# An adaLN block with linear attention and a GEGLU FFN on one core: the first token pair of the down projection, and where VectorE's extra work stands in the FFN units

## The chip, the cores and the metric

The kernel runs on one core of a Trainium2 chip. The metric is the device time of one execution in microseconds (us), the median of several runs. The profile shows one more execution, taken by the hardware profiler.

## The reference

```python
x = A_x                                    # [1, 2048, 1024], bf16
sa, ca, ga, sb, cb, gb = split(silu(c) @ w_mod, 6)
h = layernorm(x) * (1 + ca) + sa
x = x + ga * linear_attention(h, wqkv, wo)           # 32 heads
h = layernorm(x) * (1 + cb) + sb
x = x + gb * ((gelu(h @ w_gate) * (h @ w_up)) @ w_down)   # 1024 -> 3584 -> 1024
return x
```

The change concerns the last two lines: the second LayerNorm's scaling, the up and gate products (the FFN units) and the down projection.

## The kernel before

Every instruction is recorded with `sch.op` or `sch.dma` on one of five in-order streams (PE is TensorE, A is ScalarE, V is VectorE, G is GpSimd, Q is SyncE, called SP in the profile). The recorder derives each wait from the bytes that an instruction reads and writes. In the stages told here each stream runs in the order in which the Python code records it. DMAs leave from SP in order, on eight lanes in turn; a DMA also waits for the one before it on its lane.

**The FFN units.** The 2048 tokens are two halves p of 1024, and each half has 14 units; a unit v (0 to 27) computes 256 of the 3584 hidden columns for 1024 tokens with a 2x2 block scheme that needs seven products instead of eight. `unit` records them in the order P1, P5, P6, P2, P7, P3, P4, each of eight matmuls (`prod`, L1464): four for gate (t = 0), four for up (t = 1). P1 and P2 are bf16 on the tokens' h2 tiles and the raw weights; the other five are fp32r on sums: `s_sum` (L1418) makes sums of h2 tiles once for each half (eight VectorE instructions for p = 1), `t_sum` (L1438) makes sums of weights for every unit. The products add up in PSUM banks BA, BE, BB, BC (0, 2, 4, 6, plus t). Between them stand, for each t:

- after P1: `pcp` (ScalarE, L1470) copies BA to BB, on which P6 then adds; for t = 1 it must wait until the held product of the unit before (below) has read that bank
- after P5: `escp` (ScalarE, L1473) copies BE to ES
- after P6: `padd` (VectorE, L1476) writes BC = BB + ES; P7 then adds on BB, so it waits for padd
- after P7: `padd` writes BE = BB + ES; P4 then adds on BB
- after P2, P7, P3, P4: `gelu` (ScalarE, L1481) and the product gelu times up, `y_out` (VectorE, L1485). The product after P4 is held: it is recorded after P1 of the next unit.

`y_store` writes y to a DRAM scratch, `scr_y`. Extra work is hung into a unit with `hook(v, k, f)`: f is recorded when product k of unit v and its own steps have been recorded. VectorE's order around a unit's border is thus: product after P7, hook 7, product after P3, t_sum, hook 4, held product, t_sum twice, hook 5, padd. The extra work is:

- `mod2` (VectorE, L754): scales h2 of the second half by cb and sb, one instruction of 512 columns for each of eight 128-row blocks dc, for h = 0 (first 512 tokens) and h = 1. The h2 tiles arrive by transposing DMAs after `ln2_rows` (hook 3 of units 1 to 8). `mod2_act` is the same on ScalarE.
- `s_sum` for the second half, and `ar_copy` (ScalarE), a copy of an h2 block
- `b_sum` (L1577; its third step on ScalarE, L1571): sums of the down projection's weights, for K pairs 0 to 7. `raw_load(k)` loads the raw weights of K pair k (bx: the first 512 output columns, wst: the last 512).

**The down projection.** y has 3584 columns: 14 K pairs k of 2 x 128. Eight token pairs j of 256 tokens (two rows s of 128) are computed in order, with 1024 output columns in two halves c. For K pairs 0 to 12 (NST = 13) the seven products are used (`dprod`: P1, P5, P6, P2, P7, P3, P4, one matmul for each K pair); the rest is plain (`plain`: two matmuls for each K pair, row and half). `dpcp` (L1644), `descp` (L1648) and `dpadd` (L1652) are pcp, escp and padd here, and `a_sum` (VectorE, L1605; number 4 on ScalarE, L1599) makes the sums of y: numbers 0 and 2 in buffer XS 0 (for P5, then P7), 1 and 3 in XS 1 (P6, then P3), 4 in XS 2 (P4). Even pairs use banks 0, 2, 4, 6, odd pairs 1, 3, 5, 7. `devac` is two VectorE steps (L1675, L1676) and the store of 128 x 512 outputs. `x1_load` brings the residual in one of seven slots.

y lies in two buffers YL (l = 0, 1), one for all pairs: `y_load(j, l, k0, k1)` (L1586) loads a range of K pairs as soon as the pair before has used that range.

In pair 0 only K pairs 0 to 5 (NEA = 6) use the seven products: their weight sums are made in the units. K pairs 6 to 13 are plain, 64 matmuls, and meanwhile VectorE makes the weight sums of K pairs 8 to 12 (`lws(n)`: the next n steps), partly over pages that held raw weights which plain matmuls must have read first. Before the change the plain matmuls stand in four blocks of 16, one for each row and half, between the products: P1, P5, P6, P2, plain(0,0), P7, P3, plain(0,1), plain(1,1), P4, plain(1,0). The last block reads y of K pairs 6 to 13 for row 1, so the loads of y for pair 1 come late there:

```python
                if j == 1:
                    y_load(1, 0, NEA, NKP, P, 256)
                    y_load(1, 1, NEA, NKP, P, 256)
                    x1_load(j, 3)
                    a_sum(0, NEA, NST)
```

Of the kernel before, what the change touches and what calls it, by code (L numbers as in the profile page):

```python
# [10 lines left out]
P = 128  # L11
# [4 lines left out]
CPG = NCH // NSG  # L16
SGW = P * CPG
NDC = D // P
# [46 lines left out]
NKP = NFP  # L65
NST = 13
# [280 lines left out]
def bass_adaLN_cond__linear_attn_block__geglu_ffn__prompt_kernel(  # L347
# [18 lines left out]
    with ExitStack() as es:  # L366
# [133 lines left out]
        def r_h2(p, h, k0=0, k1=NDC, s0=0, s1=SGW):  # L500
            return r_t8(OFF_H2[p][h], f"h2{p}{'ab'[h]}", k0, k1, s0, s1)
# [243 lines left out]
        def h2ap(ph, dc, s0, s1):  # L745
            return H2[ph[0]][ph[1]][:, dc, s0:s1]
# [30 lines left out]
        def mod2(p, h, c0, n, dc0=0, dc1=NDC):  # L777
            mods(h2ap, r_h2p, (p, h), sc2, c0 * P, (c0 + n) * P, dc0, dc1, "h2")

        def mod2_act(h, c0=0, n=CPG, dc0=0, dc1=NDC):  # L780
            s0, s1 = c0 * P, (c0 + n) * P
            for dc in range(dc0, dc1):
                sA, sB, rs_ = sc2(dc)
                ap = h2ap((0, h), dc, s0, s1)
                sch.op(A, lambda e, ap=ap, sA=sA, sB=sB: e.activation(ap, ap, ACTF.Identity, bias=sB, scale=sA),
                       rd=r_h2(0, h, dc, dc + 1, s0, s1) + rs_, wr=r_h2(0, h, dc, dc + 1, s0, s1), note=f"h2modb {h}.{dc}")


        MC0 = 496
# [496 lines left out]
        def pq_scale(sg, h, gs):  # L1286
            i, t0 = sg % 2, h * HW
            for g0, g1 in gs:
                ap = PQ[sg][:, g0:g1, t0:t0 + HW]
                rng = r_pq(sg, g0, g1, t0, t0 + HW)  # L1290
                sch.op(V, lambda e, ap=ap, i=i, h=h, g0=g0, g1=g1: e.tensor_tensor(ap, ap, RB[i][:, h, g0:g1, :], ALU.mult),
                       rd=rng + r_rb(i, h, g0, g1), wr=rng, deps=rb_ops[sg, h], note=f"pqs{sg}.{h}.{g0}")
# [109 lines left out]
        def ar_copy(p):  # L1402
            for k in (0, 2):
                sch.op(A, lambda e, k=k: e.activation(A22R[p][:, k:k + 2, :], H2[p][1][:, ND2 + k:ND2 + k + 2, :], ACTF.Copy),
                       rd=r_h2(p, 1, ND2 + k, ND2 + k + 2), wr=r_ar(p, k, k + 2), note=f"arcp {p}.{k}")
# [17 lines left out]
        def t_sum(u, k):  # L1423
            if k == 3:
                ap, rd = wq(u, 1, 1)
                for t in range(2):
                    sch.op(A, lambda e, t=t: e.activation(TP[3][:, t, :, :], ap[:, t, :, :], ACTF.Copy), rd=rd[t:t + 1], wr=r_tp(3, t, t + 1), note=f"brcp u{u}")
                return
            if k == 0:
                (in0, r0), (in1, r1) = wq(u, 0, 1), wq(u, 0, 0)  # L1430
            elif k == 1:
                (in0, r0), (in1, r1) = wq(u, 1, 1), (T32[0], r_tp(0))
            elif k == 2:
                (in0, r0), (in1, r1) = wq(u, 1, 1), wq(u, 0, 1)
            else:
                (in0, r0), (in1, r1) = wq(u, 1, 0), (T32[1], r_tp(1))
            for t in range(2):
                sch.op(V, lambda e, t=t: e.tensor_tensor(TP[k][:, t, :, :], in0[:, t, :, :], in1[:, t, :, :], ALU.subtract),  # L1438
                       rd=r0[t:t + 1] + (r1[t:t + 1] if len(r1) == 2 else [(r1[0][0] + t * 2048, r1[0][0] + (t + 1) * 2048, r1[0][2])]),
                       wr=r_tp(k, t, t + 1), note=f"tsum{k} u{u}")  # L1440
# [58 lines left out]
        def hook(v, k, fn):  # L1499
            HK.setdefault((v, k), []).append(fn)  # L1500
# [179 lines left out]
        def cb1():  # L1680
# [6 lines left out]
                6: lambda: (mod2(0, 0, 0, 2), x_dma(10, 12)),  # L1687
                7: lambda: (t_sum(0, 0), t_sum(0, 1), pq_scale(2, 1, GH[0] + GH[1]), x_dma(12, 14)),
                8: lambda: mod2(0, 0, 2, 2),
                9: lambda: (pq_scale(3, 0, GH[0] + GH[1]), t_sum(0, 3), mod2_act(1, 0, 2), mod2_act(1, 2, 2, ND2)),  # L1690
                10: lambda: (t_sum(0, 4), t_sum(0, 2), rb_load(3, (1,)), x_dma(14, 16), row_load(GBB, R_GBB, 2, 0, "gbb", o_gb[0]), wt_dma(1)),
                11: lambda: None,
                12: lambda: (s_sum(0, 0, 0), mod2(0, 1, 2, 2, 0, ND2)),
# [18 lines left out]
            hook(v, 3, lambda c_=c_: ln2_rows(c_))  # L1712
        for i in range(4):
            hook(i + 1, 2, lambda i=i: x1_store(i))
        for h, (v, k) in enumerate(((5, 5), (9, 4))):
            hook(v, k, lambda h=h: mod2(1, h, 0, 4, 0, ND2))
        for h, v in enumerate((6, 10)):
            hook(v, 5, lambda h=h: mod2(1, h, 0, 4, ND2, NDC))
        hook(11, 3, lambda: ar_copy(1))
        for n in range(8):  # L1720
            i, j = divmod(n, 2)
            hook(10 + (n + 1) // 2, (4, 5)[n % 2], lambda i=i, j=j: s_sum(1, i, j))
        hook(12, 2, lambda: raw_load(0))
        hook(13, 2, lambda: raw_load(1))
        ew = b_sums(range(NEA + 2))
        for n in range(4 * NEA):
            v = 14 + (n + 1) // 2
            hook(v, (4, 5)[n % 2], lambda: next(ew)())
            if n % 4 == 3 and 2 + n // 4 < NEA:
                hook(v, (4, 5)[n % 2], lambda n=n: raw_load(2 + n // 4))  # L1730
        hook(16, 2, lambda: y_load(0, 0))
        hook(17, 2, lambda: y_load(0, 1))
        hook(18, 2, lambda: raw_load(13))
        hook(24, 2, lambda: raw_load(6))
        hook(26, 2, lambda: raw_load(7))
        hook(26, 4, lambda: next(ew)())
        V_ = 2 * NFP - 1
        hook(V_, 1, lambda: next(ew)())
        hook(V_, 5, lambda: a_sum(0, 0, NEA))
        hook(V_, 5, lambda: next(ew)())  # L1740
        hook(V_, 6, lambda: (raw_load(8), a_sum(1, 0, NEA), a_sum(4, 0, NEA)))
# [13 lines left out]
        def lws(n):  # L1755
            for _ in range(n):
                next(lw)()

        H = (NST + 1) // 2
        NP = S // 256  # L1760
        prev = None
        for j in range(NP):
            ns = NEA if j == 0 else NST
            lastj = j == NP - 1
            dprod(j, 1, 0, ns)
            dpcp(j)
            if j:
                devac(j - 1, 3)
                if j == 1:
                    y_load(1, 0, NEA, NKP, P, 256)  # L1770
                    y_load(1, 1, NEA, NKP, P, 256)
                    x1_load(j, 3)
                    a_sum(0, NEA, NST)
                    a_sum(1, NEA, NST)
                    a_sum(4, 0, NEA)
                    a_sum(4, NEA, NST)
                else:
                    for l in range(2):
                        y_load(j, l, NST, NKP)
                    x1_load(j, 3)  # L1780
                    a_sum(4, 0, H)
                    a_sum(4, H, NST)
            if j == 1:
                dprod(j, 5, 0, NEA)
                dprod(j, 2, 0, NEA)
                dprod(j, 5, NEA, NST)
            else:
                dprod(j, 5, 0, ns)
            descp(j)
            if j == 0:  # L1790
                a_sum(2, 0, ns)
                lws(3)
            else:
                a_sum(2, 0, H)
                a_sum(2, H, NST)
                if j < NP - 1 and j > 0:
                    y_load(j + 1, 0, 0, NST)
            dprod(j, 6, 0, ns)
            dpadd(j, BC)
            if j == 0:  # L1800
                a_sum(3, 0, ns)
            else:
                a_sum(3, 0, H)
                a_sum(3, H, NST)
            dprod(j, 2, NEA if j == 1 else 0, ns)
            plain(j, 0, 0, ns, NKP)
            if j == 0:
                y_load(1, 0, 0, NEA)
                y_load(1, 1, 0, NEA)
                lws(4)  # L1810
            elif not lastj:
                y_load(j + 1, 1, 0, NST)
            dprod(j, 7, 0, ns)
            dpadd(j, BE)
            devac(j, 0)
            if not lastj:
                for n in range(3):
                    x1_load(j + 1, n)
            if j == 0:
                a_sum(0, 0, NEA)  # L1820
                lws(4)
            elif not lastj:
                a_sum(0, 0, H)
                a_sum(0, H, NST)
            dprod(j, 3, 0, ns)
            plain(j, 0, 1, ns, NKP)
            if j == 0:
                y_load(1, 0, NEA, NKP, 0, P)
                y_load(1, 1, NEA, NKP, 0, P)
                a_sum(1, 0, NEA)  # L1830
                devac(j, 1)
                lws(4)
            else:
                devac(j, 1)
                if not lastj:
                    a_sum(1, 0, H)
                    a_sum(1, H, NST)
            plain(j, 1, 1, ns, NKP)
            if j == 0:
                lws(5)  # L1840
            devac(j, 2)
            if not lastj:
                dprod(j, 4, 0, ns)
                plain(j, 1, 0, ns, NKP)
            else:
                dprod(j, 4, 0, ns, 448)
                plain(j, 1, 0, ns, NKP, c1=448)
                plain(j, 1, 0, 0, NKP, b=BB + 1 - j % 2, c0=448, c1=512)
                devac(j, 3, 0, 448)
                devac(j, 3, 448, 512, b=BB + 1 - j % 2)  # L1850
# [76 lines left out]
```

## Time and profile before

| what | value |
|---|---|
| median of 3 runs | 797.11 us (795.54 to 797.56) |
| profiled execution, its time | 796.86 us |
| its span, first to last instruction | 795.0 us |
| granted TensorE clock, mean | 0.995 |
| FFN units (L1464 lines) | about 242 to 605 us |
| down projection (L1611 lines) | 605 to 792 us |

The span leaves out 1.9 us of the execution's time. In the profile, PE is TensorE's matmuls, PEld its weight loads, DVE is VectorE, ACT ScalarE, SP SyncE. A line number is that of the recorded instruction, so a helper's line stands for all its uses. In a timeline line the first two numbers are the start and the length in us, "xN" is the number of instructions, and the bracket tells the idle time before and what ended it.

### The profile page before, as it was taken

To read this page: it belongs to the slowest core of one execution; us is meant where nothing else is said; L and a number is where in the kernel's file an instruction comes from. 1 tells how busy PE (TensorE), PEld (TensorE's weight loads), DVE (VectorE), ACT (ScalarE), POOL (GpSimd) and SP (SyncE) were. 2 spreads that over 40 slices of the span, in tenths; PEclk is the share of its full clock that TensorE was granted. 3 is DMA by queue.
4 is the path that set the end of the run, shared out by engine and by line. 5 is a ranking of instruction groups with operands and counts; after the bars stand their busy time and mean duration, and the time that the engine had idled before them with its cause. 6 is when DMAs were issued, how large, how long until landed. Compare 5 with 4: busy or idle time off the path is not lost.

```text
span 795.0 us, 11012 instructions
## 1 busy us (share of the span) xinstructions
PE 778.6 (98%) x3840; PEld 497.5 (63%) x3904; DVE 637.5 (80%) x1080; ACT 341.6 (43%) x579; POOL 43.8 (6%) x126
## 2 busy tenths in 40 slices
PE   7999999999999999999999999999999989999998
PEld 4444445666445677667666777767776466666766
DVE  6799899983599887978999988888898756676664
ACT  2597743332683567575454445444454101111110
POOL 2121200000220001010000000000000000000000
PEclk9999999999999999999999999999999989999999
DMA  9789849737595477645354477545538333434340
GB/s 279 250 178 234 174 114 238 191 84 134 137 249 148 133 217 237 167 125 154 106 160 138 127 216 220 159 123 143 145 95 251 98 118 123 144 108 139 110 142 27
DMA packets 214127, 125.93 MB, mean 158 GB/s; under 512 B 74668, under 2 KB 204468, under 8 KB 214072
## 3 DMA queue, kind: packets, MB, share of 16 engines
q1 hardware_dynamic: 214056, 125.23, 58.3%
q8 instruction: 31, 0.51, 0.3%
q14 instruction: 24, 0.20, 0.1%
q10 hardware_dynamic: 16, 0.00, 0.0%
HBM read 88.35 MB, written 23.22 MB: 140 GB/s over the span
## 4 chain that ended last, share of the span: by engine, by line
PE 93%; DVE 3%; DMA 3%; issue 1%; SPq 0%; ACT 0%; DVEq 0%; ACTq 0%
PE ps_all L1464 43%; PE ps_all L1611 22%; PE ps_all L965 7%; PE ps_all L1299 7%; PE ps_all L914 6%; PE ps_all L929 6%; DMA mtb<-mb 1%; DMA wmq<-in_w_mod_dram 1%; DVE ps_all L1476 1%; DMA yl<-scr_y 1%; PE ps_all L947 0%; PE ps_all L1230 0%; PE ps_all L798 0%; DVE x1s L1676 0%; DVE ps_all L1675 0%
## 5 line engine op out<-in xcount | busy, mean ns | idle before, releaser
L1464 PE MATMUL ps_all<-ss,tp 128*128 128x512 f32 x896 | 225.9, 403 | 0.9 <-ACT ps_all L1470 0.6
L1464 PEld LDWEIGHTS ps_all<-ss,tp 128*128 128x128 f32 x896 | 167.4, 188 | 44.1 <-DVE ps_all L1476 3.5
L1611 PE MATMUL ps_all<-bt,xs 128*128 128x512 f32 (+1 forms) x485 | 122.1, 406 | 4.0 <-DVE xs L1605 4.0
L1481 ACT ACTIVATE ge<-ps_all 128x512 f32<-128x512 f32 x112 | 66.8, 596 | 134.5 <-DVE ps_all L1476 83.9
L1611 PEld LDWEIGHTS ps_all<-bt,xs 128*128 128x128 f32 x485 | 93.1, 192 | 26.3 <-DVE xs L1605 4.5
L1485 DVE TENSOR_TENSOR yr<-ge,ps_all 128x512 bf16<-128x512 f32 x112 | 76.8, 686 | 33.5 <-ACT ge L1481 15.5
L1438 DVE TENSOR_TENSOR tp<-wt 128x512 fp32r<-128x512 bf16 x112 | 72.1, 685 | 5.8 <-PE ps_all L1464 5.8
L1476 DVE TENSOR_TENSOR ps_all<-ps_all,es 128x512 f32<-128x512 f32 x112 | 72.3, 691 | 1.6 <-PE ps_all L1464 1.1
L1438 DVE TENSOR_TENSOR tp<-wt,tp 128x512 fp32r<-128x512 bf16 x112 | 72.0, 683 | 0.0
L1611 PE MATMUL ps_all<-bx,yl 128*128 128x512 bf16 (+2 forms) x269 | 57.3, 360 | 0.7
L965 PE MATMUL ps_all<-h1T,wq 128*128 128x512 bf16 x256 | 56.7, 379 | 0.0
L914 PE MATMUL ps_all<-wk,h1T 128*128 128x512 bf16 x239 | 55.3, 379 | 1.1 <-DVE h1T L754 0.6
L1299 PE MATMUL ps_all<-w,pq 128*128 128x512 bf16 x251 | 55.9, 379 | 0.4
L1464 PE MATMUL ps_all<-ar,tp 128*128 128x512 f32 x224 | 55.3, 389 | 0.0
L1644 ACT ACTIVATE ps_all<-ps_all 128x512 f32<-128x512 f32 x8 | 4.7, 582 | 116.8 <-PE ps_all L1611 116.8
L903 ACT ACTIVATE eb<-ps_all 128x512 f32<-128x512 f32 x64 | 36.4, 593 | 36.6 <-PE ps_all L914 14.8
L1464 PE MATMUL ps_all<-h21a,wt 128*128 128x512 bf16 x210 | 50.0, 380 | 1.0
L1464 PE MATMUL ps_all<-h20a,wt 128*128 128x512 bf16 x210 | 50.0, 380 | 0.9
L1464 PEld LDWEIGHTS ps_all<-ar,tp 128*128 128x128 f32 x224 | 42.0, 188 | 8.8
L1470 ACT ACTIVATE ps_all<-ps_all 128x512 f32<-128x512 f32 x56 | 32.6, 582 | 26.1 <-PE ps_all L1464 15.2
L965 PEld LDWEIGHTS ps_all<-h1T,wq 128*128 128x128 bf16 x256 | 25.0, 98 | 30.0
L1299 PEld LDWEIGHTS ps_all<-w,pq 128*128 128x128 bf16 x256 | 24.8, 98 | 30.2 <-issue 0.5
(145 smaller groups left out, 900.4 us busy)
## 6 DMA issues: line engine op xcount, KB each, us to landing
wt<-in_B_w_gate_dram SPq DMA_DIRECT2D x28, 512.0 KB, 4.1
wt<-in_B_w_up_dram SPq DMA_DIRECT2D x28, 512.0 KB, 5.0
scr_y<-yr SPq DMA_DIRECT2D x56, 256.0 KB, 2.9
yl<-scr_y SPq DMA_DIRECT2D x12, 832.0 KB, 4.3
wmst<-in_w_mod_dram SPq DMA_DIRECT2D x6, 1024.0 KB, 5.7
wmq<-in_w_mod_dram SPq DMA_DIRECT2D x8, 512.0 KB, 6.3
rb<-scr_rd SPq DMA_DIRECT2D x32, 128.0 KB, 3.0
scr_x<-xall SPq DMA_DIRECT2D x4, 1024.0 KB, 7.3
```

Source lines behind the costliest of these rows:

```text
L903: sch.op(A, lambda e: e.activation(EB[i][:, :], PS(bank), ACTF.Exp), prd=pr(bank), wr=rng, note=f"{note}.exp")
L914: o = sch.op(T, lambda e, dc=dc: e.matmul(PS(bank), H1[sg][:, ci, dc, :], W_[:, dc, jg * 512:(jg + 1) * 512], start=(dc == 0), stop=(dc == ...
L929: o = sch.op(T, lambda e, c_=c_: e.matmul(PS(bank, 0, n), PK[c_][:, g * P:(g + 1) * P], xrow(c_, o_, o_ + n), start=(c_ == 0), stop=(c_ == ...
L965: o = sch.op(T, lambda e, dc=dc: e.matmul(PS(b), WQ[:, dc, qc * P:(qc + 1) * P], H1[sg][:, :, dc, :], start=(dc == 0), stop=(dc == NDC - 1 ...
L1299: last[half] = sch.op(T, lambda e, g=g, half=half: e.matmul(PS(b0 + half), PQ[sg][:, g, ci * P:(ci + 1) * P], W2[:, g, half * 512:(half + ...
L1438: sch.op(V, lambda e, t=t: e.tensor_tensor(TP[k][:, t, :, :], in0[:, t, :, :], in1[:, t, :, :], ALU.subtract), rd=r0[t:t + 1] + (r1[t:t + ...
L1464: o = sch.op(T, lambda e, l_=l_, r_=r_, dc=dc: e.matmul(PS(b), l_, r_, start=fresh and dc == 0, stop=dc == ND2 - 1, skip_group_check=True) ...
L1470: sch.op(A, lambda e: e.activation(PS(BB + t), PS(BA + t), ACTF.Copy), prd=pr(BA + t), pwr=pr(BB + t), note="pcp")
L1476: sch.op(V, lambda e: e.tensor_tensor(PS(dst + t), PS(BB + t), ES[t][:, :], ALU.add), prd=pr(BB + t), rd=r_2k(OFF_ES[t], f"es{t}"), pwr=pr ...
L1481: sch.op(A, lambda e: e.activation(GE[i][:, :], PS(b), ACTF.Gelu_apprx_tanh), prd=pr(b), wr=r_2k(OFF_GE[i], f"ge{i}"), note="gelu")
L1485: sch.op(V, lambda e: e.tensor_tensor(YR[:, 2 * (v % 2) + l, h * SGW:(h + 1) * SGW], GE[i][:, :], PS(b + 1), ALU.mult), rd=r_2k(OFF_GE[i], ...
L1611: pend_ = sch.op(T, lambda e, l_=l_, r_=r_, i=i: e.matmul(PS(b, c0, c1), l_, r_, start=fresh and i == 0, stop=i == n - 1, skip_group_check ...
```

## The change

It does four things.

1. Pair 0 first does all seven products of K pairs 0 to 5, one after another, and then the 64 plain matmuls K pair by K pair: eight for each, two in each of the four banks.
2. The y of pair 1 is loaded in small steps, each after the last plain matmul of pair 0 that reads that range: K pairs 6-7, 8-9, 10-11, 12, 13, besides 0-5 as before. The sums of y for pair 1 are recorded in pieces as well (0 to 5, 6 and 7, 8 to 12), between the weight sums.
3. The evacuation (`devac`) of pair 0 moves into pair 1. From pair 2 on nothing differs.
4. In the units, the extra work of the second half moves from hooks 4 and 5 to hooks 7 and 4. The scaling of h2 for h = 0 goes in four parts of two blocks (units 5 and 6). For h = 1 it moves to unit 9: five blocks on VectorE, three on ScalarE (`mod2_act` gets the half as an argument). `ar_copy` moves from unit 11 to unit 10.

```diff
-        for h, (v, k) in enumerate(((5, 5), (9, 4))):
-            hook(v, k, lambda h=h: mod2(1, h, 0, 4, 0, ND2))
-        for h, v in enumerate((6, 10)):
-            hook(v, 5, lambda h=h: mod2(1, h, 0, 4, ND2, NDC))
-        hook(11, 3, lambda: ar_copy(1))
+        for n in range(4):
+            hook(5 + n // 2, (7, 4)[n % 2], lambda n=n: mod2(1, 0, 0, 4, 2 * n, 2 * n + 2))
+        hook(9, 7, lambda: mod2(1, 1, 0, 4, 0, 3))
+        hook(9, 4, lambda: mod2(1, 1, 0, 4, 3, 5))
+        hook(9, 6, lambda: mod2_act(1, 1, 0, 4, 5, 6))
+        hook(9, 3, lambda: mod2_act(1, 1, 0, 4, 6, 8))
+        hook(10, 3, lambda: ar_copy(1))
         for n in range(8):
             i, j = divmod(n, 2)
-            hook(10 + (n + 1) // 2, (4, 5)[n % 2], lambda i=i, j=j: s_sum(1, i, j))
+            hook(10 + n // 2, (7, 4)[n % 2], lambda i=i, j=j: s_sum(1, i, j))
...
         for n in range(4 * NEA):
-            v = 14 + (n + 1) // 2
-            hook(v, (4, 5)[n % 2], lambda: next(ew)())
+            v, k = 14 + n // 2, (7, 4)[n % 2]
+            hook(v, k, lambda: next(ew)())
             if n % 4 == 3 and 2 + n // 4 < NEA:
-                hook(v, (4, 5)[n % 2], lambda n=n: raw_load(2 + n // 4))
+                hook(v, k, lambda n=n: raw_load(2 + n // 4))
...
+        hook(26, 7, lambda: next(ew)())
         hook(26, 4, lambda: next(ew)())
         V_ = 2 * NFP - 1
-        hook(V_, 1, lambda: next(ew)())
...
+        dprod(0, 1, 0, NEA)
+        dpcp(0)
+        dprod(0, 5, 0, NEA)
+        descp(0)
+        a_sum(2, 0, NEA)
+        lws(3)
+        dprod(0, 6, 0, NEA)
+        dpadd(0, BC)
+        a_sum(3, 0, NEA)
+        dprod(0, 2, 0, NEA)
+        for l in range(2):
+            y_load(1, l, 0, NEA)
+        dprod(0, 7, 0, NEA)
+        dpadd(0, BE)
+        dprod(0, 3, 0, NEA)
+        dprod(0, 4, 0, NEA)
+        lws(6)
+        for k in range(NEA, NKP):
+            for s_ in range(2):
+                for c in range(2):
+                    plain(0, s_, c, k, k + 1)
+            for k0, k1 in {7: ((6, 8),), 9: ((8, 10),), 11: ((10, 12),), 12: ((12, 13),), 13: ((13, 14),)}.get(k, ()):
+                for l in range(2):
+                    y_load(1, l, k0, k1)
+            if k == 7:
+                a_sum(0, 0, NEA)
+                a_sum(1, 0, NEA)
+            elif k == 9:
+                lws(4)
+            elif k == 11:
+                lws(4)
+                a_sum(0, NEA, 8)
+        lws(3)
+        a_sum(0, 8, NST)
+        a_sum(1, NEA, NST)
+        for n in range(3):
+            x1_load(1, n)
+        for j in range(1, NP):
             lastj = j == NP - 1
-            dprod(j, 1, 0, ns)
+            dprod(j, 1, 0, NST)
             dpcp(j)
...
+            if j == 1:
+                a_sum(4, 0, NEA)
+                a_sum(4, NEA, NST)
+                devac(0, 0)
+                devac(0, 1)
...
+            halves(2)
...
             if j == 1:
+                devac(0, 2)
+            dprod(j, 6, 0, NST)
             dpadd(j, BC)
+            halves(3)
+            if j == 1:
+                devac(0, 3)
```

(`halves(i)` records `a_sum(i, 0, 7)` and `a_sum(i, 7, 13)`, as before for pairs 1 to 7.)

More of the change, by code (lines that the diff above doesn't have):

```diff
@@ L778, in mod2, with mod2_act @@
             mods(h2ap, r_h2p, (p, h), sc2, c0 * P, (c0 + n) * P, dc0, dc1, "h2")
-        def mod2_act(h, c0=0, n=CPG, dc0=0, dc1=NDC):
+        def mod2_act(p, h, c0=0, n=CPG, dc0=0, dc1=NDC):
             s0, s1 = c0 * P, (c0 + n) * P
@@ L783, in mod2_act @@
                 sA, sB, rs_ = sc2(dc)
-                ap = h2ap((0, h), dc, s0, s1)
+                ap = h2ap((p, h), dc, s0, s1)
                 sch.op(A, lambda e, ap=ap, sA=sA, sB=sB: e.activation(ap, ap, ACTF.Identity, bias=sB, scale=sA),
-                       rd=r_h2(0, h, dc, dc + 1, s0, s1) + rs_, wr=r_h2(0, h, dc, dc + 1, s0, s1), note=f"h2modb {h}.{dc}")
+                       rd=r_h2(p, h, dc, dc + 1, s0, s1) + rs_, wr=r_h2(p, h, dc, dc + 1, s0, s1), note=f"h2modb {h}.{dc}")
         MC0 = 496
@@ L1689, in bass_adaLN_cond__linear_attn_block__geglu_ffn__prompt_kernel @@
                 8: lambda: mod2(0, 0, 2, 2),
-                9: lambda: (pq_scale(3, 0, GH[0] + GH[1]), t_sum(0, 3), mod2_act(1, 0, 2), mod2_act(1, 2, 2, ND2)),
+                9: lambda: (pq_scale(3, 0, GH[0] + GH[1]), t_sum(0, 3), mod2_act(0, 1, 0, 2), mod2_act(0, 1, 2, 2, ND2)),
                 10: lambda: (t_sum(0, 4), t_sum(0, 2), rb_load(3, (1,)), x_dma(14, 16), row_load(GBB, R_GBB, 2, 0, "gbb", o_gb[0]), wt_dma(1)),
@@ L1760, in bass_adaLN_cond__linear_attn_block__geglu_ffn__prompt_kernel, with halves @@
         NP = S // 256
-        prev = None
-        for j in range(NP):
-            ns = NEA if j == 0 else NST
+        def halves(i):
+            a_sum(i, 0, H)
+            a_sum(i, H, NST)
+        dprod(0, 1, 0, NEA)
[11 more added lines that the diff above has]
+        dprod(0, 7, 0, NEA)
@@ L1764, in bass_adaLN_cond__linear_attn_block__geglu_ffn__prompt_kernel @@
+        lws(3)
[4 more added lines that the diff above has]
+        for j in range(1, NP):
             lastj = j == NP - 1
-            dprod(j, 1, 0, ns)
+            dprod(j, 1, 0, NST)
             dpcp(j)
-            if j:
-                devac(j - 1, 3)
[L1769 to L1782, printed above, removed]
@@ L1783, in bass_adaLN_cond__linear_attn_block__geglu_ffn__prompt_kernel @@
-            if j == 1:
[L1784 to L1798, printed above, removed]
@@ L1799, in bass_adaLN_cond__linear_attn_block__geglu_ffn__prompt_kernel @@
-            dpadd(j, BC)
[L1800 to L1811, printed above, removed]
+            if j == 1:
[3 more added lines that the diff above has]
+                devac(0, 1)
+            else:
+                devac(j - 1, 3)
+                for l in range(2):
+                    y_load(j, l, NST, NKP)
+                a_sum(4, 0, H)
+                a_sum(4, H, NST)
@@ L1812, in bass_adaLN_cond__linear_attn_block__geglu_ffn__prompt_kernel @@
+            x1_load(j, 3)
+            dprod(j, 5, 0, NST)
+            descp(j)
+            halves(2)
+            if not lastj:
+                y_load(j + 1, 0, 0, NST)
+            if j == 1:
+                devac(0, 2)
+            dprod(j, 6, 0, NST)
+            dpadd(j, BC)
+            halves(3)
+            if j == 1:
+                devac(0, 3)
+            dprod(j, 2, 0, NST)
+            plain(j, 0, 0, NST, NKP)
+            if not lastj:
                 y_load(j + 1, 1, 0, NST)
-            dprod(j, 7, 0, ns)
+            dprod(j, 7, 0, NST)
@@ L1818, in bass_adaLN_cond__linear_attn_block__geglu_ffn__prompt_kernel @@
                     x1_load(j + 1, n)
[L1819 to L1840, printed above, removed]
+                halves(0)
+            dprod(j, 3, 0, NST)
+            plain(j, 0, 1, NST, NKP)
+            devac(j, 1)
+            if not lastj:
+                halves(1)
+            plain(j, 1, 1, NST, NKP)
             devac(j, 2)
             if not lastj:
-                dprod(j, 4, 0, ns)
-                plain(j, 1, 0, ns, NKP)
-            else:
-                dprod(j, 4, 0, ns, 448)
-                plain(j, 1, 0, ns, NKP, c1=448)
+                dprod(j, 4, 0, NST)
+                plain(j, 1, 0, NST, NKP)
+            else:
+                dprod(j, 4, 0, NST, 448)
+                plain(j, 1, 0, NST, NKP, c1=448)
                 plain(j, 1, 0, 0, NKP, b=BB + 1 - j % 2, c0=448, c1=512)
```

## The prediction

> **What bounds the kernel now.** I read the page first, then TensorE's waits, then the chain in order of time, then windows and timelines around each gap. Engine totals from the page:
>
> ```profile
> PE 778.6 (98%) x3840; PEld 497.5 (63%) x3904; DVE 637.5 (80%) x1080; ACT 341.6 (43%) x579; POOL 43.8 (6%) x126
> ```
>
> TensorE is the bound, and the change adds and removes no matmul: it can only act on the gaps between them. TensorE's waits name one large gap, and the chain shows it and some small ones:
>
> ```profile
> PE ps_all L1611 <- DVE xs L1605: 4.0, 1, 4.0
> ```
> ```profile
> 318.93 1.03 DVE h21a L754 x3
> 319.96 1.22 DVE ps_all L1476 x2
> ...
> 332.20 0.73 DVE h21a L754 x2
> 332.93 1.22 DVE ps_all L1476 x2
> ...
> 633.00 4.02 DMA yl<-scr_y
> 637.12 1.10 DVE xs L1605
> ```
>
> At 633 the chain leaves TensorE for the y load of pair 1, then VectorE's sum from it. The windows there (length, then PE, PEld, DVE, ACT, POOL busy, then granted clock) show a second loss:
>
> ```profile
> 634.30:638.20 3.90, 0.00 (x0) 0.00 (x0) 1.08 (x1) 0.95 (x1) 0.00 (x0) 0.90 0.69 153
> 638.20:644.80 6.60, 6.54 (x16) 5.18 (x17) 3.15 (x4) 0.60 (x1) 0.00 (x0) 0.54 0.17 33
> ```
>
> After 3.9 us of idleness the clock was 0.54 for 6.6 us. The whole loss is read from the copy after P1 (L1644), which starts at 631.63 in pair 1, 660.94 in pair 2 and 772.11 in pair 7. Pairs 2 to 7 are thus (772.11 - 660.94) / 5 = 22.23 us apart and pairs 1 and 2 29.31: **7.1 us lost** (3.97 idle, the rest clock).
>
> Small gaps, in the FFN units: undisturbed ones start 12.60 us apart. By P1's start times, unit 5 took 13.24, 6 took 12.99, 10 took 12.98 and 12 took 13.09: 0.64 + 0.39 + 0.38 + 0.49 = **1.9 us**. There VectorE's extra work (h2 scaling at L754, s_sum) stands ahead of padd (L1476), and P7 waits for padd. The stall is the padd's start after P1, minus 5.9: starts at 6.55, 6.28, 6.25 and 6.41 us give the four within 0.02.
>
> **The change, part by part.** Matmul rates: 0.216 us for bf16 and 0.229 for fp32r fit a unit (16 and 40: 12.62, seen 12.60), a steady pair (34 and 65: 22.23, seen 22.23) and the stretch from pair 0's P1 to pair 1's (83 and 30: 24.80, seen 24.89).
>
> *Extra work moved inside the units.* Below are VectorE's timeline around the start of unit 17 (P1 at 517.04), whose only extra work is one weight sum in each of the old places, and ScalarE's second copy of P1's result (pcp):
>
> ```profile
> 515.06 1.51 DVE L1485 TENSOR_TENSOR yr<-ge,ps_all 128x512 bf16<-128x512 f32 x2
> 516.49 1.28 DVE L1438 TENSOR_TENSOR tp<-wt 128x512 fp32r<-128x512 bf16 x2
> 517.69 0.68 DVE L1577 TENSOR_TENSOR bt<-wst,bx 128x512 fp32r<-128x512 bf16 x1
> 518.29 0.68 DVE L1485 TENSOR_TENSOR yr<-ge,ps_all 128x512 bf16<-128x512 f32 x1
> 518.89 1.28 DVE L1438 TENSOR_TENSOR tp<-wt,tp 128x512 fp32r<-128x512 bf16 x2
> 520.66 1.29 DVE L1438 TENSOR_TENSOR tp<-wt 128x512 fp32r<-128x512 bf16 x2 [0.48 <-PE ps_all L1464]
> 522.47 1.30 DVE L1476 TENSOR_TENSOR ps_all<-ps_all,es 128x512 f32<-128x512 f32 x2
> ```
> ```profile
> 519.07 0.58 ACT L1470 ACTIVATE ps_all<-ps_all 128x512 f32<-128x512 f32 x1 [0.37 <-DVE yr L1485]
> ```
>
> The new places are between the two products of the first line (hook 7) and where L1577 now stands (hook 4); hook 5, next to padd, becomes empty. What comes behind them is the held product (518.29), and for that waits the copy of 519.07, and for that P6's second matmul, due 8 x 0.216 + 9 x 0.229 = 3.79 us after P1. So the move takes work off one deadline and puts it before another.
> - h2 scaling, pair 0 (units 5 and 6): two scalings, 0.7 us, in each place. Timelines of units with LayerNorm work (unit 8) show VectorE idle 0.90 and 0.76 us just there. Nothing is delayed: 0.64 and 0.39 go.
> - h2 scaling, second half (unit 9): 1.0 and 0.7 us on VectorE, three go to ScalarE, each between 0.58 (256 wide, L785) and 1.24 us (1024 wide, L689); 0.75 is taken. They read transposes issued at 366.59 that land 3.1 us later, at 369.7; ScalarE reaches the first of them at 369.4 and its next gelu isn't due before 371.28. The two later ones push gelu to about 1.9 us after P1 and the copy to an end at 3.3: inside 3.79. Unit 10's 0.38 goes.
> - s_sum, 1.13 us apart at best, now two ahead of the held product. From the end of the first product, 1.37 us before P1: 1.13, product 0.61, two sums 1.20, 1.13 bring the held product to 2.70 and its end to 3.38; the copy runs 3.48 to 4.06, and P6's second matmul waits until about 4.11 instead of 3.79: **0.32 us in each of units 11 to 14, +1.3**. Bounds: 0 if it overlaps by more, 0.5 if one more hop counts. The old 0.49 of unit 12 goes. Moving ar_copy to unit 10 delays gelu to 2.3, which 2.70 covers.
> - Weight sums (0.61 apart): the same count gives a copy that ends at 3.03: no cost. Raw weight loads leave SP half a unit earlier, behind a sum that is done.
>
> Units: -1.9 + 1.3 = **-0.6**.
>
> *Pair 0's products without plain matmuls between.* The lines that matter, VectorE and TensorE:
>
> ```profile
> 608.13 0.96 DVE L1605 TENSOR_TENSOR xs<-yl 128x768 fp32r<-128x768 bf16 x1 [0.96 <-PE ps_all L1611]
> ...
> 610.94 0.69 DVE L1652 TENSOR_TENSOR ps_all<-ps_all,es 128x512 f32<-128x512 f32 x1
> ```
> ```profile
> 609.54 4.70 PE L1611 MATMUL ps_all<-bx,yl 128*128 128x512 bf16 x21
> ```
>
> The 609.54 group is P2 (6) and 16 plain matmuls; with these moved away P2 ends at 609.54 + 1.30 = 610.84, while padd, behind a_sum and three weight sums as before, ends at 611.63. P7 waits for it: **+0.86** with the hop. P3 (its sum ends at 612.5) and P4 (padd at 613.9) then find theirs ready. Short gaps cost no clock: 0.59 us of idleness at 266 left it at 1.00.
>
> *Small y loads.* Let t0 be the end of the plain matmuls of K pair 12. P1 of pair 1 begins 1.73 later and reaches k = 12 at t0 + 4.3; P5 reaches k = 8 at 6.4. The last pieces that matter are 64 KB:
>
> ```profile
> yl<-scr_y SPq DMA_DIRECT2D x2, 64.0 KB, 2.3
> ```
>
> SP holds only those loads there (six issues more, 0.45 us each; the output stores, which held it 8.9 us at 623.50, come later). Two issues and the landing: t0 + 3.1. Bounds 2.8 and 7.1 (landings of y loads run from 1.9 to 6.1). The a_sum over five k takes 0.8: ready at 3.9 against 6.4. VectorE's weight sums fit before: about 18 us of work from 608 and pair 0 ends at 605.24 + 23.29 + 0.86 = 629.4. The last, over a page that K pair 12 read, ends at t0 + 0.8.
>
> *Pair 0's evacuation moves into pair 1.* Queued behind the two sums on VectorE: four steps (2.8), two a_sums (1.9), one evacuation (1.4), padd (0.7); from 3.1 + 1.9 they end at t0 + 11.8, P7 of pair 1 is due at 13.7. So a landing up to 1.9 us later is free. SP waits for the stores until 15.5, then loads pair 2's second y by 20.3; its sums end at 25.5, its P6 is due at 29.7. **The 7.1 us go.**
>
> Sum: -7.1 + 0.9 - 0.6 = -6.8. On the profiled execution (span 795.0, time 796.86) that is 788.2 and 790.1; on the median of 797.11, **790.3**.
>
> **Rivals.**
> 1. Units keep nothing (s_sum free) or P7 doesn't wait: 797.1 - 7.1 - 1.9 + 0.9 = 788.9 for the first, 788.0 for both. For it: the 0.32 is a difference of small hops. Chance 0.2.
> 2. The handover keeps a stall of 1 to 3 us (a landing at the long end, VectorE's queue late by more than 1.9): 791.3 to 793.3; above 3 us the clock drops as well (3.1 more). Against: three rows give the margin. Chance 0.15; that most of the gain is lost so, leaving 795 to 799, 0.03.
> 3. Slower: SP gets to the last y piece so late that TensorE idles as now and the clock falls. It decides when that landing is beyond t0 + 5.0 + 6.8 - 3.1 = 8.7; at t0 + 11 the gap is 6, with clock 9.1, and the time 799.4. For: SP serves in order and each piece waits for TensorE and a lane. Against: all loads ahead are free by then. Chance 0.04.
> 4. The plain matmuls change the PSUM bank every two instead of every sixteen. If TensorE then loses its clock, 64 x 0.216 = 13.8 us run at 0.5 and cost 13.8 more: 804. P5, P6, P7, P3 and P4 of a unit change bank at every matmul at 0.229 us and a clock of 1.00 (page, all slices of that stage), so I give it 0.02. The Trainium skill's page "TensorE: Matmul & The Clock Gate", section on psum-queue depth-cycling, reports such re-throttling when each iteration cycles through banks; by that rule the time would be this rival's, and the units' rows speak against it.
>
> **How the numbers follow.** The forecast has 0.56, with its own range 789.3 to 791.6. What a measurement can tell from no change is about 0.3%, 2.4 us. Faster: 0.56 + 0.2 + 0.15 = 0.91; same 0.03; slower 0.06. The range goes from both small terms gone (788.0) to a 2.7 us stall at the handover (793.0).
>
> **What would show it.** TensorE's waits without L1611 on xs; granted clock 1.00 from 600 to 660; pair 1 to pair 2 22.2 us by the L1644 copies; P7 of pair 0 waiting 0.9 us on L1652's line; units 5, 6 and 10 at 12.6 and 11 to 14 at 12.9. Wrong would be a y wait in TensorE or VectorE after K pair 12, longer units from 15 on, or a clock below 1 in pair 0.

## The result, and the profile after

The changed kernel takes **791.25 us** (median of 4 runs, 790.65 to 791.75) against 797.34 for the kernel before in the same set of runs: a ratio of 0.9928, interval 0.991 to 0.9945. That is 6.1 us less; 6.8 had been forecast, and the time forecast was 790.3. The profiled execution has a span of 788.8 us against 795.0, and took 790.65 us.

TensorE's waits after the change, the two lines that concern these stages (total, times, longest):

```profile
PE ps_all L1611 <- DVE ps_all L1652: 0.9, 1, 0.9
PE ps_all L1464 <- ACT ps_all L1470: 0.6, 1, 0.6
```

The 4.0 us wait for the sum of y is gone. In its place stands the wait of pair 0's P7 for padd. (The 0.6 us belong to unit 1 and were there before.) The windows over the handover from pair 0 to pair 1, with the columns as in the prediction:

```profile
626.00:636.00 10.00, 10.00 (x47) 5.95 (x46) 6.31 (x9) 3.30 (x5) 0.00 (x0) 1.00 0.37 111
636.00:646.00 10.00, 10.00 (x46) 6.98 (x45) 7.22 (x10) 0.10 (x1) 0.00 (x0) 1.00 0.62 189
```

TensorE is busy throughout and the granted clock (the third number from the end) stays at 1.00. The copies after P1 of pairs 0, 1 and 2, from ScalarE's timeline:

```profile
606.52 0.58 ACT L1644 ACTIVATE ps_all<-ps_all 128x512 f32<-128x512 f32 x1 [0.34 <-PE ps_all L1611]
632.53 0.58 ACT L1644 ACTIVATE ps_all<-ps_all 128x512 f32<-128x512 f32 x1 [5.49 <-PE ps_all L1611]
...
654.75 0.58 ACT L1644 ACTIVATE ps_all<-ps_all 128x512 f32<-128x512 f32 x1 [18.65 <-PE ps_all L1611]
```

They are 26.01 and 22.22 us apart, before 24.89 and 29.31: 1.1 lost in pair 0, 7.1 won in pair 1. The units, by P1's start times: 5, 6 and 10 now take 12.60 to 12.63 us, and units 11 to 14 take 13.03, 13.04, 13.03 and 13.03.

### The profile page after: what moved, and what is told of

Same layout as the page of the kernel before. It is cut to its first block, busy times and chain, and to the rows that moved or that the text cites. A ratio compares the mean times of both kernels' runs of the same rounds, so it can differ in the third digit from the quotient of the medians.

```text
span 788.8 us, 11024 instructions
## 1 busy us (share of the span) xinstructions
PE 775.3 (98%) x3840; PEld 495.6 (63%) x3904; DVE 636.1 (81%) x1078; ACT 342.5 (43%) x582; POOL 43.9 (6%) x126
## 5 line engine op out<-in xcount | busy, mean ns | idle before, releaser
L1611 PE MATMUL ps_all<-bt,xs 128*128 128x512 f32 (+1 forms) x485 | 118.5, 399 | 0.9 <-DVE ps_all L1652 0.9
L1611 PEld LDWEIGHTS ps_all<-bt,xs 128*128 128x128 f32 x485 | 91.1, 188 | 22.3 <-DVE ps_all L1652 1.4
L1611 PE MATMUL ps_all<-bx,yl 128*128 128x512 bf16 (+2 forms) x269 | 59.8, 360 | 0.7
```

The costliest lines, as they stand in the source:

```text
L1611: pend_ = sch.op(T, lambda e, l_=l_, r_=r_, i=i: e.matmul(PS(b, c0, c1), l_, r_, start=fresh and i == 0, stop=i == n - 1, skip_group_check ...
```

## The experiments

### The two parts, each alone

The first kernel has the change's places of the extra work in the units and the down projection of before. The second has the new down projection and the old places.

> Only the extra work inside the units is moved; the down projection is that of before. Theory (the parts are independent, and two s_sums ahead of the held product cost each of units 11 to 14 0.43 us, as in the trace of the changed kernel): units 5, 6, 10 at 12.6 us, units 11 to 14 at 13.03, so -1.9 + 1.7 = -0.2 us against before, 797.1; the 7.1 us between pairs 0 and 2 stay. Rival (the extra work is worth its whole 1.9 us, and the 0.43 comes from something else in the changed kernel): 795.4.

Measured: 795.87 us against 795.88 for the kernel before beside it, ratio 0.9999 (0.9989 to 1.0009). Units 5, 6 and 10 take 12.60 to 12.66, units 11 to 14 take 13.02 to 13.06, and the copies of pairs 1 and 2 are 28.76 us apart. So this part of the change wins about as much as it loses.

> Only the down projection is changed; the extra work stands in the units as before. Theory (independent parts): units 5, 6, 10, 12 long as before, the 7.1 us go and P7 of pair 0 waits 0.9: about -6.0 us, 791.3, the same as the whole change. Rival (the moved weight sums and h2 work are what frees VectorE for the handover): a wait for VectorE or for y comes back at pair 1 and the time is 793 or more.

Measured: 791.01 us, ratio 0.9938 (0.9925 to 0.9952), 4.9 us below the kernel before beside it. The copies are 26.00 and 22.22 us apart, as in the changed kernel, and units 5, 6, 10 and 12 are long as before. The parts are independent in the traces, and the down projection carries the gain.

### Pair 0's first padd ahead of the weight sums

```diff
         a_sum(2, 0, NEA)
-        lws(3)
         dprod(0, 6, 0, NEA)
         dpadd(0, BC)
         a_sum(3, 0, NEA)
+        lws(3)
```

> The changed kernel, with the three weight sums that stand ahead of pair 0's first padd moved behind it and behind the next sum of y. Theory (these three sums alone make P7 wait): TensorE's wait for L1652 goes, the two L1644 copies of pairs 0 and 1 are 24.9 to 25.1 us apart instead of 26.0, the time falls by 1.0 to about 790.2. Rival (VectorE's queue is full, so the sums only come late elsewhere, at the second padd or at the handover): unchanged, 791.2.

Measured: 790.11 us. The copies of pairs 0 and 1 are 25.33 us apart, 0.7 less than in the changed kernel, not 1.0. TensorE's timeline shows why:

```profile
610.21 3.12 PE L1611 MATMUL ps_all<-bt,xs 128*128 128x512 f32 x12
613.51 1.67 PE L1611 MATMUL ps_all<-bt,xs 128*128 128x512 f32 x6 [0.18 <-DVE ps_all L1652]
```

P7's wait is gone, but the three sums now stand ahead of the second padd, and P4 waits for that. The bracket's 0.18 us counts from the modelled end of the matmul before. P3's last matmul starts at 612.94, so P4, due 0.23 later, is 0.34 late. The theory holds for P7; the rival holds for about two fifths of the sum, since a kernel without either wait (e7, below) has 24.85 us between the copies.

### One s_sum behind the held product

```diff
-            hook(10 + n // 2, (7, 4)[n % 2], lambda i=i, j=j: s_sum(1, i, j))
+            hook(10 + (n + 1) // 2, (7, 1)[n % 2], lambda i=i, j=j: s_sum(1, i, j))
```

> The changed kernel, with the second s_sum of each unit moved from hook 4 (ahead of the held product) to hook 1 of the next unit (behind the held product and one pair of weight sums, ahead of the sums that wait for P5). The amount of work for each unit is the same. Theory (the held product, the copy that waits for it and P6 are the deadline): units 11 to 14 at 12.60 to 12.65 instead of 13.03, about -1.6 us, 789.6. Rival (two s_sums are simply too much VectorE work for these units): units 11 to 14 stay near 13.0, 791.2.

Measured: 789.32 us (789.05 to 789.51). Unit 12 of the changed kernel, the held product on VectorE, pcp's second copy on ScalarE, P5 and P6 on TensorE:

```profile
404.81 0.68 DVE L1485 TENSOR_TENSOR yr<-ge,ps_all 128x512 bf16<-128x512 f32 x1
```
```profile
405.58 0.58 ACT L1470 ACTIVATE ps_all<-ps_all 128x512 f32<-128x512 f32 x1 [1.81 <-DVE yr L1485]
```
```profile
403.66 4.43 PE L1464 MATMUL ps_all<-ss,tp 128*128 128x512 f32 x16
```

The same unit with the s_sum moved, ScalarE and TensorE:

```profile
404.02 0.58 ACT L1470 ACTIVATE ps_all<-ps_all 128x512 f32<-128x512 f32 x1 [0.37 <-DVE yr L1485]
```
```profile
403.54 4.00 PE L1464 MATMUL ps_all<-ss,tp 128*128 128x512 f32 x16
```

With the same work, the copy waits 0.37 us instead of 1.81 and the 16 matmuls take 4.00 instead of 4.43. Units 12 to 14 take 12.60. Unit 11 still loses 0.48, between P2 and the next P1, where ar_copy delays gelu, and with it the held product and all that VectorE does behind it up to padd. So it is the order, not the amount.

### The y loads late, and the evacuation early

The first kernel loads y of K pairs 6 to 12 in one piece behind the last plain matmul. The second puts all four evacuations ahead of pair 1's last sums.

```diff
-            for k0, k1 in {7: ((6, 8),), 9: ((8, 10),), 11: ((10, 12),), 12: ((12, 13),), 13: ((13, 14),)}.get(k, ()):
+            for k0, k1 in {13: ((NEA, NST), (NST, NKP))}.get(k, ()):
...
-                a_sum(0, NEA, 8)
         lws(3)
-        a_sum(0, 8, NST)
+        a_sum(0, NEA, NST)
```

> The changed kernel, in the same order of matmuls, but y of K pairs 6 to 12 for pair 1 is loaded in one piece (two loads) after pair 0's last plain matmul instead of in small steps. Theory (the small steps are what removes the gap): the loads issue at about 629.6, land 4.3 to 4.5 us later at about 634.5, P1 of pair 1 stops at k = 6 (due at 630.8) for 3 us or more, and the clock may fall again: 794 to 797 us, with a wait on a y load or its sum back in TensorE's rows. Rival (the order of the products or the later evacuation is what removed the gap): 791.2.

Measured: 791.99 us (ratio to before 0.994, 0.9928 to 0.9953). The theory missed: TensorE waited for a load of y only once, for 0.4 us (P7's 0.9 us for padd are there as before), and the copies of pairs 0 and 1 are 26.63 us apart, 0.6 more than with small loads.

```profile
628.93 2.52 SPq L1586 DMA_DIRECT2D yl<-scr_y  x4
```
```profile
632.51 1.69 PE L1611 MATMUL ps_all<-bx,yl 128*128 128x512 bf16 x7 [0.42 <-DMA yl<-scr_y]
```

SP issued the load as soon as K pair 12 had been read, 1.7 us earlier than the expectation had it, and it landed some 3.5 us later. P1's first six K pairs cover nearly all of that. The small loads alone aren't what removed the gap.

```diff
         lws(3)
+        for n in range(4):
+            devac(0, n)
         a_sum(0, 8, NST)
...
```

Pair 1 then has none of the four.

> The changed kernel, with all four evacuations of pair 0 put back ahead of pair 1's last sums of y on VectorE. Theory (VectorE's order at the handover has the 2 us or so of room that the prediction gave, not 5.6): the evacuations run from about 629.7 to 635.3, the sum over five k ends at 636.1, P5 of pair 1 stops at k = 8 (due at 634.0) for about 2.1 us, the time is about 793.3 and the clock stays at 1.00. Rival (where the evacuation stands is indifferent): 791.2.

Measured: 792.52 us (ratio 0.9946, 0.9932 to 0.9959). TensorE stops inside P5, and the copies of pairs 1 and 2 are 23.33 us apart, 1.1 more:

```profile
637.89 4.37 PE L1611 MATMUL ps_all<-bt,xs 128*128 128x512 f32 x18 [0.81 <-DVE xs L1605]
```

The place and the kind of wait were right, the size half: VectorE began the evacuations at 631.40, about 0.9 us before the last plain matmul was through (632.26), since the four banks end one after another.

### The load's place on SP

With late loads at 0.6 and early evacuation at 1.1 us, neither accounts for 7.1. The chain of waits of the kernel before, between the two pieces shown in the prediction, names what stands ahead of the load:

```profile
629.93 0.69 DVE x1s L1676
...
631.33 0.70 DVE x1s L1676
...
632.09 0.33 SPq L1677
...
632.52 0.39 SPq L1586
```

The load (L1586) was issued only when SP had issued the store (L1677) of the fourth evacuation, which waited for VectorE's weight sums and evacuations. The y that it overwrites had been read about 4 us earlier. The next kernel is the one before with only that order changed; no matmul moves.

```diff
                 if j == 1:
-                    y_load(1, 0, NEA, NKP, P, 256)
-                    y_load(1, 1, NEA, NKP, P, 256)
                     x1_load(j, 3)
...
             if j == 0:
                 lws(5)
-            devac(j, 2)
+            else:
+                devac(j, 2)
             if not lastj:
                 dprod(j, 4, 0, ns)
                 plain(j, 1, 0, ns, NKP)
+                if j == 0:
+                    y_load(1, 0, NEA, NKP, P, 256)
+                    y_load(1, 1, NEA, NKP, P, 256)
+                    devac(j, 2)
```

> The kernel before, order of matmuls unchanged. Only the last two y loads of pair 1 (row 1, K pairs 6 to 13) are recorded right behind pair 0's last plain matmuls and ahead of the store of the third evacuation; before, they stood on SP behind the stores of the third and the fourth. Theory (after the late one-piece load had cost only 0.6 us: what made the gap was the load's place on SP behind stores that wait for VectorE's weight sums and evacuations): the loads issue at about 628.6 and 629.1 instead of 632.5 and 633.1, land by 632.8, the sum is ready at 633.9 when P5 needs it at 634.3: no gap, clock 1.00, pairs 1 and 2 22.2 to 22.7 us apart (L1644), time within 1 us of the changed kernel's, 790 to 791. Rival (y of row 1 is read until the end of pair 0, so the order of the matmuls must change): a gap of 2 us or more remains, 793 or more.

Measured: 790.33 us (789.84 to 791.09), ratio 0.9917 (0.9904 to 0.993). SP and VectorE:

```profile
628.66 0.99 SPq L1586 DMA_DIRECT2D yl<-scr_y  x2
630.72 1.75 SPq L1677 DMA_DIRECT2D out_dram<-x1s  x2
```
```profile
632.96 1.09 DVE L1605 TENSOR_TENSOR xs<-yl,yl 128x896 fp32r<-128x896 bf16 x1 [0.91 <-DMA yl<-scr_y]
```

The loads leave at 628.66 instead of 632.52, the sum starts at 632.96 instead of 637.12, and TensorE finds it ready. VectorE's third evacuation starts at 629.16, before at 629.13, so VectorE didn't get free any earlier. The copies of pairs 0, 1 and 2 are 24.88 and 22.35 us apart. All but about 0.1 us of the gap's cost went with the order of matmuls unchanged, and P7's wait did not come.

The opposite test takes the changed kernel, with the order of matmuls that it has, and puts the loads, in one piece, behind the stores of all four evacuations:

> The changed kernel, order of matmuls unchanged, with the four evacuations of pair 0 ahead of pair 1's last sums and the y loads of K pairs 6 to 13 in one piece behind their stores on SP. Each alone had cost 0.6 and 1.1 us. Theory (load behind store behind VectorE is the gap): the stores hold the loads until about 635, they land near 638.7, P1 of pair 1 stops at k = 6 (due at 630.8) for 7 us or more, the clock falls again: 800 to 803. Rival (the two are independent, so their costs add): about 793.

Measured: 801.85 us, ratio 1.0059 (1.0046 to 1.0073), slower than the kernel before. TensorE's longest wait, and its windows (length, busy, clock, DMA share, GB/s):

```profile
PE ps_all L1611 <- DMA yl<-scr_y: 7.6, 1, 7.6
```
```profile
636.00:638.00 2.00, 0.00 (x0) 0.50 0.92 220
638.00:640.00 2.00, 1.32 (x4) 0.50 1.01 369
640.00:642.00 2.00, 2.00 (x5) 0.50 0.58 197
642.00:644.00 2.00, 2.00 (x9) 0.94 0.00 0
```

By the copies, the late loads alone cost 0.6 us and the early evacuation alone 1.1; together they cost 9.5 (35.27 and 22.49 us apart), and 10.4 by the times. A load behind a store behind VectorE is the gap, and the halved clock comes back with it.

> The changed kernel once more, as the measure for the two beside it on the same chip: 791.2 us by the earlier result.

Measured beside these two: 791.49 us (790.93 to 793.63), ratio 0.9935 (0.9921 to 0.9948).

### The gap filled

```diff
                 dprod(j, 2, 0, NEA)
+                for _ in range(14):
+                    dmm(BA, True, [ya(0, 0, 0)], [(BXT[0][:, 0, :], r_bx(0, 0, 1))], "fill")
```

> The kernel before, with 14 matmuls of no use (3.0 us, into a bank that pair 0 has given up) put into the gap of 4 us at the handover. Theory (the gap costs twice, once as idleness and once as a clock that is halved some 3 us into it): the idle rest is about 1 us, the granted clock stays at 1.00, and the time falls by the clock's part, 1.5 to 3 us, to 793 to 794.4, with less spread between runs. Rival (only idleness counts, or the clock falls anyway): 795.9.

Measured: 794.86 us against 797.16, ratio 0.9974 (0.9964 to 0.9984). The windows (columns as in the prediction) and TensorE's timeline:

```profile
634.00:639.00 5.00, 4.25 (x20) 1.75 (x18) 0.91 (x1) 0.95 (x1) 0.00 (x0) 1.00 0.65 151
```
```profile
639.24 4.83 PE L1611 MATMUL ps_all<-bt,xs 128*128 128x512 f32 x20 [0.99 <-DVE xs L1605]
```

Matmuls of no use make the kernel 2.3 us faster: the next product still starts when the sum is there, but at full clock. The copies of pairs 1 and 2 are 26.57 us apart instead of 29.31, so in these two profiles the clock's part of the gap is 2.7 us.

### The best versions

> The changed kernel with three things moved: the second s_sum of each unit to hook 1 of the next unit, ar_copy from behind P3's gelu to behind P2's (where ScalarE sat idle 2.9 us), and the three weight sums ahead of pair 0's first padd behind its second padd. Theory: units 5 to 15 all at 12.60 to 12.66, the first two L1644 copies 24.9 to 25.0 us apart, no wait for padd: -1.7 - 1.1, about 788.4. Rival (the moved weight sums come too late at the handover): 789 to 790, with a wait at pair 1's P5 or P6.

Measured: 788.92 us (788.05 to 789.87), ratio 0.99 (0.9886 to 0.9914). All units from 5 on take 12.60 to 12.64, the copies are 24.85 and 22.22 us apart, and no wait for padd is left. It is 2.3 us below the changed kernel's 791.25, which was measured in another set of runs.

> The order of matmuls and the down projection of the kernel before with only the y loads moved ahead of the store, and in the units the places of the change with the second s_sum at hook 1 and ar_copy behind P2's gelu. Theory (the parts are independent): 2.0 us below the kernel with only the loads moved, 788.3; units 5 to 15 at 12.60 to 12.66, L1644 copies of pairs 0, 1 and 2 24.9 and 22.3 us apart; as fast as the changed kernel with three things moved, which has none of the old order. Rival (the changed order of pair 0 is worth something of its own): 789 or more.

Measured: 788.42 us (788.20 to 790.12), ratio 0.9906 (0.9892 to 0.9921). The copies are 24.89 and 22.36 us apart. Within what these runs can tell, the old order of pair 0 with the loads in their right place is as fast as the new order.

## Why the prediction was right, and where it wasn't

- **Scaling of h2 (0.64, 0.39 and 0.38 go).** Right: units 5, 6 and 10 take 12.60 to 12.63. Unit 12's old 0.49 gave way to the loss of the next point.
- **s_sum, 0.32 us in each of units 11 to 14.** Right in its chain and mis-sized at its end. The held product was put 2.70 us after P1 and starts at 404.81 - 402.11 = 2.70; the copy was put at 3.48 to 4.06 and runs from 3.47 to 4.05; P6's second matmul was put at 4.11 and starts at 406.22, 4.11 after P1 and 0.30 late. What the sum left out comes behind it: the next matmul starts at 406.55, 0.33 us later instead of 0.23. So a unit loses 0.43 instead of 0.32, and the four lose 1.7 us instead of 1.3. The split shows that this chain is the cause.
- **P7 of pair 0 waits 0.86 us.** Right in its start and mis-sized in its cost. P7 starts 6.45 us after P1 (605.01, 611.46), forecast from padd's end were 6.46. But the stretch between the copies grew by 1.12. The group at 609.54, on which the 0.86 rests, has 22 matmuls (6 and 16), and its line shows x21: the record of P2's first is missing. In e7's trace, where P2's six are all there, P2 starts 4.08 us after P1, in that line 4.30:

```profile
605.40 1.47 PE L1611 MATMUL ps_all<-bx,yl 128*128 128x512 bf16 x6
606.52 3.12 PE L1611 MATMUL ps_all<-bt,xs 128*128 128x512 f32 x12
609.48 1.47 PE L1611 MATMUL ps_all<-bx,yl 128*128 128x512 bf16 x6
```

So P2 ends 0.22 us earlier than was read, and P7 is 1.06 us late. Another 0.1 comes behind it, as in the units. That the wait shown, 0.90, is so near to 0.86 is chance: it counts from the modelled end of P2's last matmul. e3's kernel gave back 0.7 of the stretch and e7's all of it.

- **The small y loads.** The forecast of their landing, 3.1 us after K pair 12, was a little late: VectorE's sum over five k starts at 630.28, 2.5 us after 627.8. The room for the evacuations was there, and so were SP's times (the load for pair 2 at 642.93, forecast 15.5 us after K pair 12, 643.3).
- **"The 7.1 us go."** They went, and the loads and VectorE's queue were in time as forecast. What the prediction didn't see is why the loads had been late. Its chain began at the DMA, at 633.00, and left out the four pieces before it. With these the cause could have been read: a load that waits on SP for stores. The prediction mentions those stores only as something that would come later, and the text ahead of it takes the last block of plain matmuls, which reads y of row 1, for the reason. The kernel before with two loads moved shows that it isn't. Small loads and a later evacuation each put the loads ahead of the stores; without one of them the changed kernel loses 0.6 or 1.1 us, without both 9.5. The new order of matmuls wins at most the 0.1 us by which e9 stays behind at the handover, and as it stands costs 1.1 in pair 0.
- **Rival 4 (banks).** The 64 plain matmuls that change the bank every two ran from 615.70 to 629.52, 0.216 us each, at a clock of 1.00. The re-throttling that the Trainium skill's page "TensorE: Matmul & The Clock Gate" reports in its section on psum-queue depth-cycling is not seen here.
- **The sum.** -7.1 + 1.1 - 1.9 + 1.7 = -6.2 by the after trace, which is the change of the span (795.0 to 788.8). The two small terms make up the difference to -6.8. In another set of runs, beside e9, the change is worth 5.55 us (797.04 to 791.49).

## What to carry to other kernels

On an in-order queue a load can wait for a store that has nothing to do with it: follow the chain back past the DMA to what its queue was doing, before reordering the compute. Moving extra work away from one deadline puts it before another, so write down the chain up to the next matmul that waits, with its durations, as was done for the held product. A gap long enough to lower the clock costs more than its length. Count the matmuls of a group in a trace against the code before taking its start for the start of the product: a missing record here hid 0.2 us.

## What the runs showed of the hardware that was not expected

The cost of the lowered clock differs from run to run. In the 11 timed runs of the kernel before beside e9, the spans go from 794.1 to 796.5 us with a mean granted clock of 0.995 to 0.998; those of the filled gap, which stays at 0.999 to 1.0, go from 792.1 to 793.7. In the profile of before TensorE fell idle at 634.3, the clock dropped at about 637.4, and it returned at about 644.3, 6.0 us after the matmuls had resumed (638.26). With the loads behind the stores it dropped 4.3 us after the last matmul (at about 635.4) and returned 3.6 us after the resumption (638.68). The Trainium skill's page "TensorE: Matmul & The Clock Gate", Part 1, gives at least one window of about 3.4 us for either way, and lets the window run free, so that it doesn't start anew with the kernel. The returns after 3.6 and 6.0 us and the drop after 4.3 agree with that, and the drop after 3.1 came a little earlier. So the 7.1 us read from one profile of before stood for 4 us of idleness and a clock loss of about 3. In e1's profile the same handover cost 6.5 (28.76 - 22.22).

A stop also costs about 0.1 us more than the lateness of the matmul that waited. Behind a stop, the second fp32r matmul starts 0.33 to 0.34 us after the first instead of 0.23: in the changed kernel at 406.22 and 406.55 and at 611.46 and 611.80, in the kernel before at 321.22 and 321.56. Why is not shown.
